# Eight token subtractions moved from GpSimd to VectorE, two issue paces changed, and the last short block's sum taken off the accumulating DMA

## The chip, the cores and the metric

The kernel runs on one core of one Trainium2 chip. The metric is the device time of one execution in microseconds (us), the median of several runs. The engines are called PE (TensorE), DVE (VectorE), ACT (ScalarE), POOL (GpSimd) and SP (SyncE, which issues most DMAs).

## The reference, cut to what matters

Three stages follow each other over 2304 tokens of width 512. A linear attention gives `x`. A gated MLP (GLU) with 1536 hidden features replaces it:

```python
xn = x / rms * rms_g
x = (silu(xn @ w_gate) * (xn @ w_val)) @ w_out
```

A plain MLP with 2048 hidden features ends it. The change lies almost wholly in this last stage:

```python
h = x @ w_in
out = silu(h) @ w_out
```

Everything is float32. The weights come as float64 and are decoded on the chip.

## The kernel before, in words

**Blocks.** The tokens lie in five blocks: 0 to 3 of 512 tokens and a short one, 4, of 256. Every float32 operand of a product is held as a high and a low half (the high half is an ACT copy to the matmul type, the low half a DVE subtraction, lines 198 and 199 for `h`), and a product runs three passes, `PASS`.

**Groups of hidden features.** `stream()` goes through `groups`: nine GLU groups of one feature tile each, then eight MLP groups of a pair of feature tiles. The first two MLP groups (here the first and second pair; `NSTD = 2`) are computed plainly, block by block, with `mlp_block` and `g1_mlp`. From the third pair on, the four long blocks go through `quad`, which forms a pair of blocks and a pair of feature tiles with seven half products instead of eight, in the manner of Strassen. For that, `quad` wants sums and differences of the two blocks of a pair ("token sums") and of the two weight tiles. Behind the two quads of a group come the short block's two products and the output rows of block 3.

**Token sums.** `token_sums(p, ...)` returns a list of small steps for block pair `p`: four additions of 128x1024 elements on DVE (`whole`, line 371), four subtractions on POOL (`less`, line 341), four high halves on ACT (`tok_high`, line 363) and four low halves on DVE (`tok_low`, line 366). It is called once for the GLU and, for the MLP, once for pair 0 in the middle of the first plain group and once for pair 1 in the middle of the second. A step that is not done when `quad` needs its result is issued there (`summed`).

**Weights.** `WeightQueue` holds jobs in a fixed order: load a float64 tile, decode it (five DVE instructions, lines 146 to 157, then two POOL additions, line 160), high half on ACT (line 438), low half on DVE (line 442), weight sums on POOL, and so on. `tick()` issues the next job if a weight slot is free. `quad` calls it at fixed places; elsewhere the loop at the end of the kernel calls it by pace. `need` issues jobs at once if a product wants a weight that is not ready.

**The pacing loop.** The stream yields an estimate of TensorE time before each product and behind each output slice (about 1.3 for a half product or an output slice of 128 tokens, 2.6 for a whole product of a long block). The loop adds it to two counters:

```python
for c in stream():
    due += c
    gone += c
    if sums and gone > wq.rest:
        sums.pop(0)()
        gone = 0.0
    if wq.hold:
        due = min(due, M_PACE)
    elif due > wq.pace and wq.tick():
        due = min(due - wq.pace, wq.pace)
```

`wq.rest` spaces the token sum steps, `wq.pace` the weight jobs. `wq.hold` is on inside a quad. `gone` is reset only where a step is issued, so it goes on growing while the list of sums is empty.

**Outputs.** `g2_mlp` computes output rows for 128 tokens at a time. Even slices leave PSUM by ACT (line 316), odd ones by DVE (line 318), and a pair is added to `out` in HBM by an accumulating DMA that POOL issues (line 323). In the last group, block 2 comes last: its rows so far are loaded from `out` beforehand (line 815), DVE adds the PSUM result to them (line 310), and SP writes them with plain DMAs (line 312); its last slice is cut in two halves. Block 4, just ahead of it, still goes by the accumulating DMA.

Of the kernel before, what the change touches and what calls it, by code (L numbers as in the profile page):

```python
# [8 lines left out]
F32 = mybir.dt.float32  # L9
# [5 lines left out]
ALU = mybir.AluOpType  # L15
# [5 lines left out]
def kernel(  # L21
# [14 lines left out]
    nc = tc.nc  # L36
# [8 lines left out]
    TB = 4  # L45
# [144 lines left out]

    PASS = [(0, 0), (0, 1), (1, 0)]
    HALVES = [slice(0, 64), slice(64, P)]
    M_PACE, A_PACE, S_PACE, R_PACE, T_PACE = 2.0, 1.8, 2.5, 1.5, 1.2
    W_EARLY, GRAIN, GATE = 3, 3, 3

    def split_h(s, j):
# [82 lines left out]
    def out_pair(j, n):  # L279
        i = j * TB + 2 * n  # L280
        kind, b, hf, r = tiles[i]
        if kind == "m":
            r0 = b * S + 256 * hf
            return [(0, P, out[r0:r0 + 256, :].rearrange("(p r) d -> p r d", r=2))]
        rows = out.rearrange("(b s) d -> s b d", s=S)[512:576]
        return [(64 * e, 64 * e + 64, rows[:, e::2, :]) for e in range(2)]

    def g2_mlp(fs, j, hs, first, last, end):
        wq.need(*[(2, "p", f) for f in fs])
        nt = blocks[j] // P  # L290
        nn = 3 * len(fs)
        cuts = [(t, 0, DM) for t in range(nt)]
        if end:
            cuts[-1:] = [(nt - 1, d, d + DM // 2) for d in (0, DM // 2)]
        for t, d0, d1 in cuts:
            ps = ps_tile("ps_y", [P, DM])[:, d0:d1]
            n = 0
            for f in fs:
                for a, c in PASS:
                    nc.tensor.matmul(  # L300
                        out=ps,
                        lhsT=hs[f][:, a, t * P:(t + 1) * P],
                        rhs=wt[2, "p", f][:, c, d0:d1],
                        start=(n == 0),
                        stop=(n == nn - 1),
                    )
                    n += 1
            if end:
                o = end[t // 2][:, t % 2, d0:d1]
                nc.vector.tensor_tensor(out=o, in0=ps, in1=o, op=ALU.add)  # L310
                for p0, p1, rows in out_rows(j * TB + t):
                    nc.sync.dma_start(out=rows[:, d0:d1], in_=o[p0:p1])
            else:
                if t % 2 == 0:
                    o = stage()
                    nc.scalar.activation(out=o[:, 0, :], in_=ps, func=AF.Copy)  # L316
                else:
                    nc.vector.tensor_copy(out=o[:, 1, :], in_=ps)  # L318
                    for p0, p1, rows in out_pair(j, t // 2):
                        if first:  # L320
                            nc.sync.dma_start(out=rows, in_=o[p0:p1])
                        else:
                            nc.gpsimd.dma_start(out=rows, in_=o[p0:p1], accum_op=ALU.add)  # L323
            yield 0.216 * nn

    KH = KC // 2
    tok, sums, ready, wait, stages = {}, [], set(), [], []
# [8 lines left out]
    def w_tile(side, slot, dtype=F32R):  # L336
        pool = pools["w"][2] if side and slot < W_EARLY else pools["w"][side]
        return pool.tile([P, 2 * KC * P], dtype, tag=f"w{side}_{slot}", name=f"w{side}_{slot}")

    def less(out, x, y, op=ALU.subtract):  # L340
        nc.gpsimd.tensor_tensor(out=out, in0=x, in1=y, op=op)
# [3 lines left out]
            sums.pop(0)()  # L345
        return lambda b, c: tok[p, n][b][:, c, :]

    def token_sums(p, temp, end):
        half = lambda j, a, h: xs[2 * p + j][:, a, KH * h:KH * (h + 1), :].bitcast(F32)
        u = {}  # L350

        def tok_high(n, x):
            if n == 1:
                tok[p, n] = [xs[2 * p + 1][:, a, :KH, :] for a in range(2)]
            elif p:
                v = big.tile([P, KC * TB * P], F32R, tag=f"ya{n - 2}", name=f"ya{n - 2}")
                v = v.rearrange("p (a c t) -> p a c t", a=2, c=KH)
                tok[p, n] = [v[:, a] for a in range(2)]
            else:
                tok[p, n] = [  # L360
                    w_tile(1, 3 + 2 * (n - 2) + a).rearrange("p (c t) -> p c t", c=KH) for a in range(2)
                ]
            nc.scalar.activation(out=tok[p, n][0], in_=x, func=AF.Copy)

        def tok_low(n, x):
            nc.vector.tensor_tensor(out=tok[p, n][1], in0=x, in1=tok[p, n][0].bitcast(F32), op=ALU.subtract)
            ready.add((p, n))

        def whole(k, j, h):
            u[k] = u[1] if k == 3 else temp(k).rearrange("p (c t) -> p c t", c=KH)  # L370
            nc.vector.tensor_tensor(out=u[k], in0=half(j, 0, h), in1=half(j, 1, h), op=ALU.add)

        ready.difference_update([(p, n) for n in range(1, 5)])
        return [
            lambda: whole(1, 1, 0),
            lambda: whole(0, 0, 0),
            lambda: less(u[0], u[1], u[0]),
            lambda: whole(2, 1, 1),
            lambda: less(u[1], u[2], u[1]),
            lambda: less(u[2], u[2], u[0]),  # L380
            lambda: tok_high(3, u[1]),
            lambda: (tok_low(3, u[1]), tok_high(2, u[2])),
            lambda: tok_low(2, u[2]),
            lambda: whole(3, 0, 1),
            lambda: less(u[3], u[3], u[2]),
            lambda: None,
            lambda: tok_high(4, u[3]),
            lambda: (tok_low(4, u[3]), end(0)),
        ], [
            lambda: tok_high(1, u[0]),  # L390
            lambda: (tok_low(1, u[0]), end(1)),
        ]
# [173 lines left out]
    wq = WeightQueue()  # L566
# [147 lines left out]
    def chain_of(*its):  # L714
        for it in its:
            yield from it

    def stream():
# [10 lines left out]
            wq.hold = n == 0  # L729
            wq.rest = T_PACE if wq.hold else M_PACE + T_PACE  # L730

        now, later = token_sums(0, temp, end)
        sums.extend(now)
        for n, (j, fs) in enumerate(order):
            hs, mine = {}, n == len(order) - 1
# [6 lines left out]
            out = g2_glu(fs, j, hs, j >= NE and fs is f0, False)  # L742
            pend = chain_of(pend, out) if mine else out
        spent = [(1, k) for k in range(3)]
        for u, (kind, fs) in enumerate(groups):
            first, last = kind == 2 and fs[0] == 0, u == len(groups) - 1
            done = u + 1 == std
            wq.rest = T_PACE + M_PACE / 2
            wq.pace = A_PACE if u < std else S_PACE if u < std + NSTD else R_PACE
            hs = {j: {} for j in range(NB)}  # L750
            if std <= u < std + NSTD:
                out_of = lambda j: g2_mlp(fs, j, hs[j], first, False, False)
# [7 lines left out]
                for n, k in enumerate(each):  # L760
# [11 lines left out]
                    j = n // 2 if first else 1 - n // 2  # L772
                    yield from mlp_block(fs[n % 2], j, hs[j], ys, k if n < 3 else (k[0], 9))
                wq.hold = False
                if first:
                    assert wq.jobs.pop(0)[0] == 1 << 10
                    now, later = token_sums(
                        0, lambda k: w_tile(1, 7, F32) if k == 2 else wq.slot(("t", k), F32), lambda n: None
                    )
# [17 lines left out]
            if kind == 1:  # L797
                f = fs[0]
                out_of = lambda j: g2_glu(fs, j, hs[j], False, done)
                ys = chain_of(out_of(0), out_of(1))  # L800
                yield from glu_block(f, 2, hs[2], ys, {"g": 0, "v": 1})
                yield from glu_block(f, 3, hs[3], ys, {"g": 1, "v": 1})
                yield from glu_block(f, 4, hs[4], ys, {"g": 1, "v": 1})
                yield from ys
                pend = chain_of(out_of(2), out_of(3), out_of(4))
                wq.release(*wq.keys(u)[0])
            else:
                out_of = lambda j, end=None: g2_mlp(fs, j, hs[j], False, last, end)
                yield from quad(u, chain_of(out_of(1), out_of(0)), hs, 1)
                if last:  # L810
                    *stages[:], o0, o1 = [w_tile(1, k, F32) for k in range(3, 9)]
                    ends = [o.rearrange("p (t d) -> p t d", t=2) for o in (o0, o1)]
                    for n, o in enumerate(ends):
                        for p0, p1, rows in out_pair(2, n):
                            nc.sync.dma_start(out=o[p0:p1], in_=rows)
                    yield from g1_mlp(fs[0], 4, hs[4], (), out_of(3))
                    yield from g1_mlp(fs[1], 4, hs[4], (), ())
                    yield from chain_of(out_of(4), out_of(2, ends))
                else:
                    yield from g1_mlp(fs[0], 4, hs[4], (), out_of(3))  # L820
                    yield from g1_mlp(fs[1], 4, hs[4], (), ())
                    wq.release(*wq.keys(u)[0])
                    pend = chain_of(out_of(2), out_of(4))
# [697 lines left out]
    with tc.manual_schedule():  # L1521
# [68 lines left out]
        for c in stream():  # L1590
            due += c
            gone += c
            if sums and gone > wq.rest:
                sums.pop(0)()
                gone = 0.0
            if wq.hold:
                due = min(due, M_PACE)
            elif due > wq.pace and wq.tick():
                due = min(due - wq.pace, wq.pace)
# [30 lines left out]
```

## Time and profile before

| | us |
|---|---|
| median of 3 runs | 970.9 |
| lowest and highest of them | 969.96, 971.26 |
| the profiled execution, its own time | 971.98 |
| its span, first to last instruction | 970.2 |
| PE busy with matmuls | 941.4 (97%) |
| DVE busy | 709.1 (73%) |
| POOL busy | 473.0 (49%) |
| ACT busy | 473.4 (49%) |

The profiled execution's own time is 1.8 us more than its span, and 1.1 us above the median of the runs. The granted TensorE clock has a mean of 0.994 of full speed. The chain of work that ended last lies on PE for 82% of the span and on DVE for 9%. From 236 to 556 us (the GLU groups) PE has no idle time; the MLP's two plain groups lie from about 556 to 664 us, its six quad groups from there to 963 us.

### The profile page before, as it was taken

What the parts mean: (1) busy time and instruction counts of PE and PEld (TensorE: products, weight loads), DVE (VectorE), ACT (ScalarE), POOL (GpSimd) and SP (SyncE); (2) the same over time, 40 slices, a digit from 0 to 9 for tenths busy, and PEclk for the clock granted to TensorE, in tenths of its full rate; (3) what the DMA queues carried; (4) which work ended last, traced back from release to release, by engine and by line L of the source; (5) the groups of instructions that cost most, each with busy time, mean ns of one, the idle gap of its engine ahead of it and who ended that gap; (6) DMA issues with size and microseconds to landing.
All of it is one profiled execution on the core that took longest, in us unless ns stands there. A gap on an engine that the chain in (4) does not pass through costs nothing.

```text
span 970.2 us, 17242 instructions
## 1 busy us (share of the span) xinstructions
PE 941.4 (97%) x6534; PEld 786.3 (81%) x6534; DVE 709.1 (73%) x1336; ACT 473.4 (49%) x1052; POOL 473.0 (49%) x474
## 2 busy tenths in 40 slices
PE   8999999999999999999999999989899999999996
PEld 6888878888888888888888877778688877878785
DVE  5998989658678777878877879778586747474633
ACT  5999876543433343333332453435445454545441
POOL 7888655315436534534534106386364546363411
PEclk9999999999999999999999999999999999999998
DMA  7655543002112112012102004475777877686667
GB/s 176 174 135 144 139 124 100 5 31 80 44 44 66 33 55 66 22 44 66 44 22 87 23 22 129 133 129 105 134 137 147 153 130 170 112 172 112 111 130 149
DMA packets 88962, 94.50 MB, mean 97 GB/s; under 512 B 28336, under 2 KB 74672, under 8 KB 88880
## 3 DMA queue, kind: packets, MB, share of 16 engines
q1 hardware_dynamic: 78816, 61.36, 22.4%
q0 software_dynamic: 9792, 31.99, 20.0%
q8 instruction: 51, 0.84, 0.4%
q14 instruction: 31, 0.25, 0.1%
q10 hardware_dynamic: 272, 0.07, 0.0%
HBM read 50.92 MB, written 37.75 MB: 91 GB/s over the span
## 4 chain that ended last, share of the span: by engine, by line
PE 82%; DVE 9%; DMA 2%; issue 2%; ACT 2%; POOL 2%; SPq 1%; DVEq 0%; POOLq 0%; ACTq 0%
PE g L572 19%; PE g L205 16%; PE y L300 16%; PE y L259 13%; PE y L205 5%; PE b L1098 3%; PE b L205 2%; DVE h L199 2%; PE b L1282 2%; PE kv L1178 2%; PE b L1071 2%; PE b L1498 1%; POOL m L160 1%; DVE w L442 1%; PE b L1258 1%
## 5 line engine op out<-in xcount | busy, mean ns | idle before, releaser
L160 POOL TENSOR_TENSOR m<-m,raw 128x512 int32<-128x512 int32 x136 | 192.4, 1415 | 211.9 <-issue 118.5
L300 PE MATMUL y<-w,h 128*128 128x512 f32 (+1 forms) x870 | 216.6, 393 | 9.6 <-DVE h L199 4.6
L300 PEld LDWEIGHTS y<-w,h 128*128 128x128 f32 x870 | 163.4, 190 | 46.8 <-DVE h L199 6.0
L205 PE MATMUL g<-xs,w 128*128 128x512 f32 x768 | 187.4, 390 | 1.4 <-DVE w L442 1.4
L205 PEld LDWEIGHTS g<-xs,w 128*128 128x128 f32 x768 | 143.3, 188 | 31.1 <-DVE w L442 1.9
L199 DVE TENSOR_TENSOR h<-s,h 128x512 fp32r<-128x512 f32 (+1 forms) x134 | 110.0, 831 | 63.9 <-ACT h L198 62.7
L259 PE MATMUL y<-h,w 128*128 128x512 f32 (+1 forms) x648 | 155.4, 366 | 0.0
L270 DVE TENSOR_TENSOR ya<-y,ya 128x512 f32<-128x512 f32 (+1 forms) x200 | 122.7, 630 | 21.0 <-PE y L259 20.8
L259 PEld LDWEIGHTS y<-h,w 128*128 128x128 f32 x648 | 113.2, 188 | 20.4 <-DVE h L199 0.5
L572 PE MATMUL g<-xs,w 128*128 128x512 f32 x504 | 128.7, 391 | 0.0
L198 ACT ACTIVATE h<-s 128x512 fp32r<-128x512 f32 (+1 forms) x134 | 77.3, 585 | 89.7 <-DVE s L684 49.4
L323 POOL DMA_DIRECT2D out_dram<-ya x64 | 59.3, 989 | 117.9 <-DVE ya L318 55.1
L572 PEld LDWEIGHTS g<-xs,w 128*128 128x128 f32 x504 | 94.3, 188 | 19.5
L318 DVE COPY ya<-y 128x512 f32<-128x512 f32 x67 | 45.9, 686 | 71.1 <-PE y L300 71.1
L1147 ACT ACTIVATE e<-b,nb 128x128 f32<-128x128 f32 x272 | 75.8, 421 | 7.9 <-issue 4.3
L442 DVE TENSOR_TENSOR w<-m,w 128x512 fp32r<-128x512 f32 x65 | 70.7, 1088 | 11.9 <-ACT w L438 10.7
L316 ACT ACTIVATE ya<-y 128x512 f32<-128x512 f32 x67 | 39.8, 593 | 71.4 <-PE y L300 70.3
L572 PE MATMUL g<-w,w 128*128 128x512 f32 x270 | 68.8, 390 | 0.0
L205 PEld LDWEIGHTS y<-xs,w 128*128 128x128 f32 x480 | 61.2, 188 | 8.9 <-ACT ya L316 6.4
L597 ACT ACTIVATE s<-s 128x512 f32<-128x512 f32 x33 | 20.9, 632 | 96.0 <-DVE s L602 96.0
L205 PE MATMUL y<-xs,w 128*128 128x256 f32 x480 | 62.5, 280 | 5.2 <-ACT ya L316 5.2
L572 PEld LDWEIGHTS g<-w,w 128*128 128x128 f32 x270 | 50.1, 188 | 10.0
(135 smaller groups left out, 1352.1 us busy)
## 6 DMA issues: line engine op xcount, KB each, us to landing
out_dram<-ya POOLq DMA_DIRECT2D x52, 512.0 KB, 6.7
raw<-in_moe_w_out_dram SPq DMA_DIRECT2D x28, 512.0 KB, 4.1
raw<-in_moe_w_in_dram SPq DMA_DIRECT2D x16, 512.0 KB, 4.3
raw<-in_moe_w_gate_dram SPq DMA_DIRECT2D x12, 512.0 KB, 3.5
raw<-in_moe_w_val_dram SPq DMA_DIRECT2D x12, 512.0 KB, 3.6
qT<-e SPq DMA_DIRECT2D x72, 64.0 KB, 2.6
x<-in_k_dram SPq DMA_DIRECT2D x16, 256.0 KB, 3.6
x<-in_q_dram SPq DMA_DIRECT2D x16, 256.0 KB, 3.3
```

The costliest lines, as they stand in the source:

```text
L160: tt(out=mi, in0=mi, in1=(low if step == 5 else high).bitcast(I32), op=ALU.add)
L198: nc.scalar.activation(out=ht[:, 0, :], in_=s, func=AF.Copy)
L199: nc.vector.tensor_tensor(out=ht[:, 1, :], in0=s, in1=ht[:, 0, :].bitcast(F32), op=ALU.subtract)
L205: nc.tensor.matmul(out=ps, lhsT=w[:, a, cc * P:(cc + 1) * P], rhs=xs[j][:, c, cc, :], start=(n == 0), stop=(n == 3 * KC - 1),)
L259: nc.tensor.matmul(out=ps, lhsT=wt[1, "o", f][:, a, d * P:(d + 1) * P], rhs=hs[f][:, c, :], start=(n == 0), stop=(n == nn - 1),)
L270: nc.vector.tensor_tensor(out=y[:, d, :], in0=ps, in1=y[:, d, :], op=ALU.add)
L300: nc.tensor.matmul(out=ps, lhsT=hs[f][:, a, t * P:(t + 1) * P], rhs=wt[2, "p", f][:, c, d0:d1], start=(n == 0), stop=(n == nn - 1),)
L318: nc.vector.tensor_copy(out=o[:, 1, :], in_=ps)
L323: nc.gpsimd.dma_start(out=rows, in_=o[p0:p1], accum_op=ALU.add)
L442: eng.tensor_tensor(out=v[:, 1, :], in0=x, in1=v[:, 0, :].bitcast(F32), op=ALU.subtract)
L572: nc.tensor.matmul(out=ps, lhsT=w[:, a, (c0 + c) * P:(c0 + c + 1) * P], rhs=x(b, c), start=(start and n == 0), stop=(n == 3 * KH - 1), ski ...
L1147: nc.scalar.activation(out=st.e[r][:, :, h, :] if blocks4 else st.e[r][:, h, :], in_=src.rearrange("p (a f) -> p a f", a=4) if blocks4 els ...
```

## The change

It moves the four subtractions of each of the MLP's two `token_sums` calls from POOL to DVE (the GLU's stay on POOL). It sets the spacing of the sum steps to 1.9 in place of 2.2 and keeps what is left of `gone` behind a step in place of setting it to zero. It sets the pace of weight jobs in the quad groups to 2.0 in place of 1.5. In the last group the short block's rows are loaded, added on DVE and written by SP as block 2's are.

```diff
-    M_PACE, A_PACE, S_PACE, R_PACE, T_PACE = 2.0, 1.8, 2.5, 1.5, 1.2
+    M_PACE, A_PACE, S_PACE, R_PACE, S_REST, T_PACE = 2.0, 1.8, 2.5, 2.0, 1.9, 1.2
...
-        if end:
+        if end and nt == TB:
             cuts[-1:] = [(nt - 1, d, d + DM // 2) for d in (0, DM // 2)]
...
-    def token_sums(p, temp, end):
+    def token_sums(p, temp, end, eng=nc.vector):
...
+        def minus(out, x, y):
+            eng.tensor_tensor(out=out, in0=x, in1=y, op=ALU.subtract)
+
...
-            lambda: less(u[0], u[1], u[0]),
+            lambda: minus(u[0], u[1], u[0]),
             lambda: whole(2, 1, 1),
-            lambda: less(u[1], u[2], u[1]),
-            lambda: less(u[2], u[2], u[0]),
+            lambda: minus(u[1], u[2], u[1]),
+            lambda: minus(u[2], u[2], u[0]),
...
-            lambda: less(u[3], u[3], u[2]),
+            lambda: minus(u[3], u[3], u[2]),
...
-        now, later = token_sums(0, temp, end)
+        now, later = token_sums(0, temp, end, nc.gpsimd)
...
-            wq.rest = T_PACE + M_PACE / 2
+            wq.rest = S_REST
...
-                    *stages[:], o0, o1 = [w_tile(1, k, F32) for k in range(3, 9)]
-                    ends = [o.rearrange("p (t d) -> p t d", t=2) for o in (o0, o1)]
-                    for n, o in enumerate(ends):
-                        for p0, p1, rows in out_pair(2, n):
+                    *stages[:], o0, o1, o2 = [w_tile(1, k, F32) for k in range(3, 9)]
+                    ends = [o.rearrange("p (t d) -> p t d", t=2) for o in (o0, o1, o2)]
+                    for o, j, n in zip(ends, (4, 2, 2), (0, 0, 1)):
+                        for p0, p1, rows in out_pair(j, n):
                             nc.sync.dma_start(out=o[p0:p1], in_=rows)
...
-                    yield from chain_of(out_of(4), out_of(2, ends))
+                    yield from chain_of(out_of(4, ends[:1]), out_of(2, ends[1:]))
...
-                gone = 0.0
+                gone = gone - wq.rest if wq.rest == S_REST else 0.0
```

## Rows read from the trace of the kernel before

**Rows 1.** Busy time in stretches: start:end, length, busy by engine, PE clock, DMA

```profile
556.00:664.00 108.00, 100.38 (x461) 82.95 (x460) 88.63 (x117) 47.23 (x82) 50.17 (x31) 0.98 0.36 93
664.00:712.00 48.00, 44.95 (x194) 36.34 (x193) 31.21 (x47) 23.16 (x39) 22.34 (x20) 0.96 0.74 137
```

**Rows 2.** What PE waited for, 575 to 963 us: total, times, longest

```profile
PE y L205 <- ACT ya L316: 5.2, 3, 1.7
PE y L300 <- DVE h L199: 4.6, 2, 2.5
PE y L300 <- DVE w L442: 2.9, 2, 2.7
PE y L300 <- DVE ya L270: 1.6, 1, 1.6
PE g L205 <- DVE w L442: 1.4, 1, 1.4
```

**Rows 3.** DVE in order of time, 582 to 603 us: start, us, what, idle before

```profile
582.03 0.68 DVE L199 TENSOR_TENSOR h<-s,h 128x512 fp32r<-128x512 f32 x1
582.63 1.22 DVE L371 TENSOR_TENSOR w<-xs 128x1024 f32<-128x1024 f32 x1
583.76 0.42 DVE L146 TENSOR_SCALAR m<-raw 128x512 uint32<-128x512 uint32 x1
...
585.10 0.42 DVE L157 TENSOR_SCALAR m<-m 128x512 uint32<-128x512 uint32 x1
586.86 0.69 DVE L318 COPY ya<-y 128x512 f32<-128x512 f32 x1 [1.33 <-PE y L300]
587.46 1.97 DVE L371 TENSOR_TENSOR w<-xs 128x1024 f32<-128x1024 f32 x1
...
595.28 5.65 DVE L199 TENSOR_TENSOR h<-s,h 128x512 fp32r<-128x512 f32 x2
```

**Rows 4.** POOL in order of time, 584 to 604 us

```profile
585.65 2.69 POOL L160 TENSOR_TENSOR m<-m,raw 128x512 int32<-128x512 int32 x2 [40.63 <-issue]
...
594.23 8.95 POOL L341 TENSOR_TENSOR w<-w,w 128x1024 f32<-128x1024 f32 x3
```

**Rows 5.** PE in order of time, 594 to 613 us

```profile
598.18 4.64 PE L300 MATMUL y<-w,h 128*128 128x512 f32 x19 [2.07 <-DVE h L199]
...
610.29 1.19 PE L205 MATMUL g<-xs,w 128*128 128x512 f32 x4 [1.45 <-DVE w L442]
```

**Rows 6.** All engines in order of time, 627 to 647 us

```profile
628.39 1.22 DVE L366 TENSOR_TENSOR xs<-w,xs 128x1024 fp32r<-128x1024 f32 x1
...
636.83 3.52 POOL L160 TENSOR_TENSOR m<-m,raw 128x512 int32<-128x512 int32 x2 [0.67 <-DVE m L157]
...
639.14 1.76 DVE L199 TENSOR_TENSOR h<-s,h 128x512 fp32r<-128x512 f32 x1
...
640.96 6.12 PE L300 MATMUL y<-w,h 128*128 128x512 f32 x19 [2.49 <-DVE h L199]
```

**Rows 7.** PE in order of time, 676 to 698 us

```profile
687.09 0.73 PE L300 MATMUL y<-w,h 128*128 128x512 f32 x2 [2.72 <-DVE w L442]
687.66 1.99 PE L572 MATMUL g<-xs,w 128*128 128x512 f32 x6
689.45 2.71 PE L300 MATMUL y<-w,h 128*128 128x512 f32 x6
692.00 1.55 PE L572 MATMUL g<-ya,w 128*128 128x512 f32 x6
```

**Rows 8.** All engines in order of time, 804 to 811 us

```profile
805.11 3.06 POOL L160 TENSOR_TENSOR m<-m,raw 128x512 int32<-128x512 int32 x2 [2.23 <-issue]
...
808.21 0.63 ACT L438 ACTIVATE w<-m 128x512 fp32r<-128x512 f32 x1 [4.00 <-POOL m L160]
...
808.74 0.58 ACT L316 ACTIVATE ya<-y 128x512 f32<-128x512 f32 x1
...
809.38 1.68 PE L205 MATMUL y<-xs,w 128*128 128x256 f32 x12 [1.72 <-ACT ya L316]
```

**Rows 9.** All engines in order of time, 936 us to the end

```profile
958.76 1.99 POOL L323 DMA_DIRECT2D out_dram<-w  x2 [3.82 <-issue]
...
959.60 5.71 SPq L312 DMA_DIRECT2D out_dram<-w  x5
...
963.03 0.42 DVE L310 TENSOR_TENSOR w<-y,w 128x256 f32<-128x256 f32 x1 [0.29 <-PE y L300]
```

**Rows 10.** Line 312's own view: its issues by SP, and their time to landing

```profile
L312 SPq DMA_DIRECT2D out_dram<-w x5: 332/344/1494, 959.6 to 964.4; - x5
...
DMA to landing us min/median/max: 3.6/4.8/5.8
```

## The prediction

> **What bounds the kernel now.** I read the page's busy times first: PE is busy for 941.4 of 970.2 us, so only its idle time and its slow stretches can be won. Next the busy time by stretches. The GLU groups leave PE no idle time. The two plain MLP groups leave 108 - 100.38 = 7.6 us idle, and the third pair's group 48 - 44.95 = 3.1 us, at a mean clock of 0.98 and 0.96 [rows 1]. Then PE's waits, which name the idle time [rows 2]: 4.6 us for low halves of `h` and 1.4 us for a weight's low half in the plain groups, 2.9 us for weights in the third pair's group, 5.2 us in three equal pieces later, for an ACT copy of `y`. The 1.6 us for `ya` are the last GLU group's, which the change doesn't touch.
>
> DVE holds PE up in the plain groups because POOL holds DVE up. A 128x1024 sum on DVE takes 1.22 us alone (1.13 to the next start), and 1.97 us where it meets POOL's pair of additions: it ends 1.1 us after that pair's end at 588.34 [rows 3, 4]. Two low halves, 0.6 us each when free, take 5.65 us beside POOL's three subtractions of 3.0 us each [rows 3, 4]. So a DVE instruction whose inputs lie in SBUF waits out the POOL instruction that is running, and the two engines take turns. The copy from PSUM at 586.86 isn't held by the same POOL pair. The Trainium skill (SBUF — State Buffer, Who interferes with whom) says the same: a VectorE instruction with two SBUF inputs and a GpSimd instruction that reads SBUF exclude each other for a whole instruction; the rows agree.
>
> **The change part by part.**
>
> *How often sums are issued.* By the text, 1.9 in place of 2.2. But `gone` isn't reset while no sums are pending. By the stream's own estimates it has grown by some 345 through the nine GLU groups when the MLP's first sum becomes ready. A step now takes only 1.9 off it and each yield gives back 1.3 or more, so the 32 steps use up at most 32 x 0.6 = 19. The spacing never bites: one step goes out at every yield, so at half products and output slices (1.3) twice as often as before. Counted along the stream, pair 0's steps end before the second plain group (before: inside it), and pair 1's before the third pair's group (before: inside it).
>
> *First plain group, term +0.4.* Between the first sum (582.63) and the low half PE waits for, DVE's queue now holds three subtractions at 1.13 = 3.4 us more, while POOL's first subtraction, about 2.7 to 3.0 us, no longer stands ahead. I walked the queue in turns: sum, decode (five instructions, 583.76 to 585.52, so 1.75), sum, copy 0.6, subtraction, sum, decode, copy, subtraction, low half 0.6, subtraction, low half, with four POOL additions of 1.35 in between. The second low half ends at 599.3; PE now goes on at 598.2 [rows 5]. The 1.2 us are mostly given back at the next stop, the weight's low half: three DVE steps (a token low half, a sum, a subtraction) now stand ahead of it, and two POOL subtractions don't. I get 610.7 against 610.3 [rows 5]. Bounds: -3.4 (both stops, 2.07 + 1.45, go) and +1.7.
>
> *Second plain group, term +3.6.* The stop before 640.96 waits for the low half at 639.14 [rows 6]. Before, DVE needs from the token low half at 628.39 to 640.9 for it: that low half, two decodes, two copies, two sums and the half itself, with four POOL additions in turn. Afterwards the token low half starts about 3.3 us earlier, at 625.1. But a weight's and an `h` low half (1.2) now follow it, and one sum and three subtractions more stand ahead of the half PE wants: 4 x 1.13 = 4.5, and 0.7 of waiting for ACT. 640.9 - 3.3 + 1.2 + 4.5 + 0.7 = 644.0, so 3.1 us later. Behind the stop PE's 19 matmuls took 6.12 us, against 4.64 for 19 after the first stop [rows 5, 6]: the granted clock drops for a while (the two stretches with such stops have means under 1 [rows 1]), which costs some 1.5 to 1.8 us; I add 0.5 for a longer stop. Bounds: -4.2 (the 2.49 us stop and its slow stretch go, if the turns with POOL cost less than walked) and +5.
>
> *Third pair's group, term -4.6.* The two stops (2.9 us) wait for low halves of the output weights [rows 2, 7]. They are late because two weight slots serve as scratch for pair 1's sums until these end: along the stream, the weight jobs find no slot free five times. With the sums done earlier only one attempt fails, and both weights are split before their product. What goes with the stops is the slow stretch behind: the two groups of six after 687.66 take until 692.00 [rows 7], with the two matmuls before them 4.9 us for 14 that take 3.2 at full clock, so 1.7 us. Bounds: 0 and -4.9.
>
> *Pace of weight jobs, term -5.2.* Behind the quads lie six yields of 1.3. With 1.5 four jobs go out in the first four, so a weight's high half reaches ACT while POOL still decodes: ACT waits 4.0 us for POOL, the copy of `y` behind it comes at 808.74, and PE, which wants that PSUM bank, stops for 1.72 us [rows 8]; three groups have this, 5.2 us [rows 2]. With 2.0 the jobs go out at yields 1, 2, 4 and 5, and the high half comes behind the copy that PE wants, one slice later. Each group issues 14 jobs, ten at fixed places in the quads and four here, before as after, so the jobs in the quads move by one place and none is forced. Their cover is the quads' slack: before, PE waits for nothing in them from 712 us on. If a moved decode does strike a low half there, it costs one turn, 1.35 us a group. Bounds: 0 and -5.5.
>
> *The end, term -0.7.* PE's order is the same to its last matmul. Two more DVE adds take the place of an ACT and a DVE copy; two POOL accumulating DMAs (958.76 to 960.75) go, and four SP writes and two loads come [rows 9]. The added writes are issued before 959.6, while SP has nothing to do; at 0.34 each [rows 10] they cost 1.4 us of its queue, hidden there. The loads run 25 us ahead. What ends the span is the last write, issued at 964.4, landing up to 5.8 us later, where the quickest takes 3.6 [rows 10]. Less beside it may win up to 2.2 us; one SP issue took 1.49, and four such would cost 1 us at the end. I take a third of the gain.
>
> Sum: 0.4 + 3.6 - 4.6 - 5.2 - 0.7 = -6.5. The profiled execution's 971.98 becomes 965.5; it stood 1.1 above the median, so the median of 970.9 becomes **964.4**.
>
> **The rivals.**
>
> *DVE is eased more than I walked.* POOL's subtractions blocked DVE by up to 3 us each and DVE's cost 1.13. If the turns with POOL's decodes overlap more with copies than I let them, the stops of the plain groups shrink: without them and the slow stretch, -7.6 in place of +4.0, so 952.8; half of that 958.6. For it: DVE is busy 88.63 of 108 us there, including its waits [rows 1]. Against: the sums now go out in bursts.
>
> *The third group or the boundary stops stay.* They would if another late job took their place: 964.4 + 4.6 = 969.0, or + 5.2 = 969.6. For it: ACT and POOL stay in order. Against: the count of jobs above.
>
> *Moving work between DVE and POOL wins nothing.* Here the plain groups would stay as they are, the sums' order included, and the rest would come: 964.4 - 4.0 = 960.4. The Trainium skill (Perfetto Trace Analysis, Optimizing Scalar/DVE Operations) warns that shifting operations between these two might not help since they share a read port. It lies inside my range.
>
> *Slower: the burst in the second plain group.* All 14 steps of pair 1 go out at 1.3 us of PE time apart, together with two decodes and `h`. If each low half of `h` there, not only the first, comes behind a sum and a POOL turn, three more stops of 2.5 us with a slow stretch of 1.8 each follow: 3 x 4.3 = 12.9, so 977.3. It decides from about 8.4 us of such stops on, two of them. Against: from 644 us on the sums still left are six DVE steps, 7 us, over more than 20 us of PE time.
>
> **How the numbers follow.** My forecast has 0.55, the eased DVE 0.19, the stops that stay 0.13, no gain from moving 0.06, the slower burst 0.07. The forecast's own bounds reach about 961 to 968. The range goes from 957.5, the better half of the eased case, to 970.0 beyond the stops that stay. A measurement of this kernel tells about 0.2%, 1.9 us, from no change, so faster means below 969.0: the forecast, the eased case, the useless move and about a third of the stops that stay, 0.83; within, 0.10; slower, 0.07.
>
> **What would show it.** In the changed profile: no 128x1024 subtraction on POOL after 236 us; sum steps at every yield; PE's stop before 641 us longer, near 5.5 us, and again a slow stretch; no wait for a weight in the third pair's group; none for the ACT copy of `y` at the groups' ends; no accumulating DMA after 955 us. I am wrong if the plain groups get shorter, if the three pieces of 1.7 us stay, or if new waits stand inside the quads.

## The result and the profile after

The changed kernel takes **959.73 us** (median of 4 runs, 959.17 to 960.5), the kernel before, beside it, 971.08 (4 runs, 969.96 to 971.91): a ratio of 0.9884, 95% interval 0.9867 to 0.9902, so 11.3 us less, where 6.5 were forecast. 959.73 lies inside the range. The profiled execution of after took 960.5, with a span of 958.7 against 970.2.

To see where the time went I cut the span at four places of PE's order. The rows of after, PE in order of time:

```profile
575.14 5.69 PE L300 MATMUL y<-w,h 128*128 128x512 f32 x24 [1.63 <-DVE ya L270]
...
664.61 2.99 PE L205 MATMUL y<-xs,w 128*128 128x256 f32 x24
...
712.84 1.58 PE L205 MATMUL y<-xs,w 128*128 128x256 f32 x12
...
944.97 1.58 PE L205 MATMUL y<-xs,w 128*128 128x256 f32 x12
```

They are the MLP's first output products, the short block's products that end the second plain group, and the short block's second product behind the third and behind the last quads. In the kernel before they start at 575.65, 660.51, 713.90 and 952.66. So the lengths in the profiled executions are, in us:

| stretch | before | after | change | forecast |
|---|---|---|---|---|
| two plain groups | 84.86 | 89.47 | +4.61 | +4.0 |
| third pair's group | 53.39 | 48.23 | -5.16 | -4.6 |
| the five groups after it | 238.76 | 232.13 | -6.63 | -5.2 |
| from there to the end | 17.54 | 13.73 | -3.81 | -0.7 |

The rest of the 11.5 us between the spans, 0.5, lies before these products. Three terms came within 1.5 us; the end won five times its forecast. The busy times by stretch, in the columns of [rows 1], show the same trade:

```profile
556.00:664.00 108.00, 98.90 (x429) 80.65 (x428) 88.94 (x126) 46.47 (x78) 32.73 (x22) 0.95 0.35 93
664.00:712.00 48.00, 47.92 (x229) 40.02 (x228) 32.08 (x51) 24.65 (x44) 24.38 (x23) 1.00 0.73 142
```

The plain groups lost 1.5 us of PE's busy time and 0.03 of clock; the third pair's group has no idle time left and full clock. PE's waits, 575 to 963 us, as in [rows 2]:

```profile
PE y L300 <- DVE h L199: 6.6, 3, 4.2
PE y L300 <- DVE ya L270: 1.6, 1, 1.6
PE y L300 <- ACT h L198: 1.1, 2, 0.8
```

All weight waits (2.9 and 1.4 us) and the three for the copy of `y` (5.2 us) are gone; the wait for `h`'s low halves grew from 4.6 to 6.6. Where it stands, PE in order of time:

```profile
596.59 0.96 PE L300 MATMUL y<-w,h 128*128 128x512 f32 x3 [1.70 <-DVE h L199]
598.32 6.20 PE L300 MATMUL y<-w,h 128*128 128x512 f32 x19 [0.78 <-DVE h L199]
...
609.91 1.55 PE L205 MATMUL g<-xs,w 128*128 128x512 f32 x6
...
638.82 0.73 PE L300 MATMUL y<-w,h 128*128 128x512 f32 x2 [0.84 <-ACT h L198]
643.72 7.43 PE L300 MATMUL y<-w,h 128*128 128x512 f32 x19 [4.16 <-DVE h L199]
```

The stop before 643.72 is the one before 640.96 [rows 6], now 4.16 us. What DVE does before it, in order of time:

```profile
624.95 1.22 DVE L366 TENSOR_TENSOR xs<-w,xs 128x1024 fp32r<-128x1024 f32 x1
...
628.37 2.35 DVE L371 TENSOR_TENSOR w<-xs 128x1024 f32<-128x1024 f32 x2
...
632.32 1.22 DVE L374 TENSOR_TENSOR w<-w,w 128x1024 f32<-128x1024 f32 x1
...
634.05 1.74 DVE L371 TENSOR_TENSOR ya<-xs 128x1024 f32<-128x1024 f32 x1
...
638.53 1.21 DVE L374 TENSOR_TENSOR w<-ya,w 128x1024 f32<-128x1024 f32 x1
...
640.27 1.71 DVE L374 TENSOR_TENSOR ya<-ya,w 128x1024 f32<-128x1024 f32 x1
641.90 1.76 DVE L199 TENSOR_TENSOR h<-s,h 128x512 fp32r<-128x512 f32 x1
```

Six 128x1024 sums and subtractions (line 374 holds the latter) stand between the token low half and the low half that PE wants: the burst. Between the corresponding rows of before [rows 6], DVE has two sums:

```profile
632.54 1.37 DVE L371 TENSOR_TENSOR w<-xs 128x1024 f32<-128x1024 f32 x1
...
637.26 1.95 DVE L371 TENSOR_TENSOR w<-xs 128x1024 f32<-128x1024 f32 x1
```

POOL's decode pair beside those of after:

```profile
638.70 4.41 POOL L160 TENSOR_TENSOR m<-m,raw 128x512 int32<-128x512 int32 x2 [0.67 <-DVE m L157]
```

It takes 4.41 us, against 2.69 when DVE lets it run [rows 4]: taking turns costs POOL as well. Behind the short block's first product of a quad group, all engines in order of time (the place of [rows 8]):

```profile
801.81 0.60 ACT L316 ACTIVATE ya<-y 128x512 f32<-128x512 f32 x1 [1.18 <-PE y L300]
...
802.30 0.62 ACT L441 ACTIVATE w<-m 128x512 fp32r<-128x512 f32 x1
...
803.32 3.02 POOL L160 TENSOR_TENSOR m<-m,raw 128x512 int32<-128x512 int32 x2 [2.23 <-issue]
...
804.53 0.60 ACT L316 ACTIVATE ya<-y 128x512 f32<-128x512 f32 x1 [1.60 <-PE y L300]
```

The weight's high half (line 441) now stands behind a copy of `y`, and the next copy waits for PE alone, not for POOL. The end, DVE's last row and line 312's own view:

```profile
955.36 0.42 DVE L310 TENSOR_TENSOR w<-y,w 128x256 f32<-128x256 f32 x1 [0.29 <-PE y L300]
```

```profile
L312 SPq DMA_DIRECT2D out_dram<-w x9: 332/372/588, 949.2 to 955.8; - x9
...
DMA to landing us min/median/max: 1.8/2.7/3.3
```

The last write is issued 0.4 us after the start of the last add (before: 1.3), and lands after 1.8 us (before: 3.6; the least in each view [rows 10]); the median landing is 2.7 us against 4.8. The rest lies behind the last landing: from it to the end of the span pass 1.1 us, before 2.3. There each engine closes the program with a `DRAIN`, and POOL's is the long one. First before, then after (of three, the shortest, middle and longest in ns, then the first and last start in us; the longest is the first):

```profile
L1625 POOLq DRAIN  x3: 40/102/10253, 959.2 to 969.9; - x3
...
L1628 POOLq DRAIN  x3: 40/93/8527, 946.4 to 958.4; - x3
```

In before it runs from 959.2 for 10.25 us, to 969.4: 2.8 us behind the landing of the last accumulating DMA (issued at 959.4, landed 7.2 us later), and 1.5 behind that of the last plain write, at 967.9. So there the span waited for POOL, not for the last write. In after POOL's `DRAIN` ends at 954.9, ahead of the last write's landing at 957.6. The pieces are 0.9, 1.8 and 1.2 us, together the 3.8 but for rounding.

### The profile page after: what moved, and what is told of

It is laid out like the page before. It is cut to its first block, busy times and chain, and to the rows that moved or that the text cites. A ratio compares the mean times of both kernels' runs of the same rounds, so it can differ in the third digit from the quotient of the medians.

```text
span 958.7 us, 17244 instructions
## 1 busy us (share of the span) xinstructions
PE 940.8 (98%) x6534; PEld 787.4 (82%) x6534; DVE 718.9 (75%) x1345; ACT 474.3 (49%) x1051; POOL 454.9 (47%) x464
## 4 chain that ended last, share of the span: by engine, by line
PE 80%; DVE 4%; ACT 1%; issue 0%; ACTq 0%
PE g L575 21%; PE y L300 20%; PE g L205 16%; PE y L259 13%; PE y L205 6%; PE b L1501 2%; PE b L205 1%; DVE h L199 1%; DVE w L374 1%; PE b L1285 1%; DVE w L371 0%; ACT h L198 0%; PE b L1381 0%; DVE ya L270 0%; ACT xs L272 0%
## 5 line engine op out<-in xcount | busy, mean ns | idle before, releaser
L160 POOL TENSOR_TENSOR m<-m,raw 128x512 int32<-128x512 int32 x136 | 196.4, 1444 | 242.7 <-issue 113.6
L199 DVE TENSOR_TENSOR h<-s,h 128x512 fp32r<-128x512 f32 (+1 forms) x134 | 117.8, 890 | 61.6 <-ACT h L198 60.5
L445 DVE TENSOR_TENSOR w<-m,w 128x512 fp32r<-128x512 f32 x65 | 67.1, 1034 | 17.9 <-ACT w L441 16.2
```

The lines of the kernel that those rows point to most:

```text
L160: tt(out=mi, in0=mi, in1=(low if step == 5 else high).bitcast(I32), op=ALU.add)
L199: nc.vector.tensor_tensor(out=ht[:, 1, :], in0=s, in1=ht[:, 0, :].bitcast(F32), op=ALU.subtract)
L445: eng.tensor_tensor(out=v[:, 1, :], in0=x, in1=v[:, 0, :].bitcast(F32), op=ALU.subtract)
```

## The experiments

Ratios are to the kernel before on the same chip, whose medians there are 969.55 to 971.06. The edits are to the kernel after unless said otherwise. The stretches of the table above, for all of them, are those of one profiled execution each; the medians are of four runs, in x1_pool and x2_pace of seven:

| kernel | plain | third | five groups | end | median, us | ratio (95%) |
|---|---|---|---|---|---|---|
| x1_pool | 93.00 | 52.94 | 232.13 | 13.68 | 967.51 | 0.9964 (0.9948 to 0.9980) |
| x2_pace | 87.95 | 47.95 | 240.98 | 13.70 | 967.81 | 0.9967 (0.9954 to 0.9981) |
| x3_tail | 89.03 | 47.84 | 232.13 | 17.61 | 962.91 | 0.9920 (0.9905 to 0.9935) |
| x4_reset | 80.78 | 53.34 | 256.44 | 13.70 | 981.76 | 1.0115 (1.0098 to 1.0132) |
| x5_early | 90.05 | 47.84 | 232.13 | 13.75 | 958.90 | 0.9874 (0.9857 to 0.9890) |
| x6_acclate | 89.32 | 48.24 | 232.14 | 17.65 | 963.34 | 0.9924 (0.9907 to 0.9940) |
| x7_nodebt | 84.03 | 47.84 | 232.13 | 13.70 | 953.93 | 0.9833 (0.9814 to 0.9852) |
| x8_comb | 86.77 | 47.85 | 232.13 | 13.69 | 955.66 | 0.9849 (0.9830 to 0.9868) |
| x9_paceonly | 84.12 | 53.80 | 256.13 | 17.35 | 988.28 | 1.0186 (1.0167 to 1.0204) |
| x10_split | 83.13 | 47.84 | 232.14 | 13.78 | 951.92 | 0.9804 (0.9787 to 0.9820) |
| x11_split2 | 82.62 | 48.10 | 232.13 | 13.75 | 953.57 | 0.9822 (0.9805 to 0.9839) |

**x1_pool: the subtractions back on POOL.**

```diff
-    def token_sums(p, temp, end, eng=nc.vector):
+    def token_sums(p, temp, end, eng=nc.gpsimd):
```

> The changed kernel with the MLP's eight subtractions back on POOL, all else as changed. Theory (DVE and POOL take turns, a POOL subtraction holds DVE 2.7 us where DVE's own takes 1.13): the plain groups get longer by 1 to 5 us, so 961 to 965 us against 959.7, likeliest 962. Rival (moving work between the two wins nothing): within 1 us of 959.7. Rival (the burst on DVE is what lengthens the plain groups): 956 to 958.

Measured: 967.51, beyond the range; the move to DVE is worth 7.8 us under the burst; of the profiled executions' difference 3.5 lie in the plain groups and 4.7 in the third pair's group, which I had not foreseen. Its waits:

```profile
PE y L300 <- DVE h L199: 8.4, 5, 3.3
PE g L205 <- DVE w L445: 3.1, 1, 3.1
PE g L575 <- ACT g L587: 2.4, 1, 2.4
```

POOL's subtractions take 2.6 to 2.8 us each here, so the sums end inside the third group: the last token low half runs on DVE at 674.33 to 676.66, a weight's high half on ACT waits for it, and the ACT copy that PE wants (line 587) comes behind. "Moving work between DVE and POOL wins nothing" falls.

**x2_pace: the pace of weight jobs back to 1.5** (`R_PACE`).

> The changed kernel with the pace of weight jobs in the quad groups back at 1.5. Theory (at 1.5 a weight's high half stands ahead of the copy that PE wants): the 1.7 us stops for ACT come back. Counted along the stream, the jobs now stand so that four groups have the bad order, not three, at 1.9 to 2.2 us each: 967.3 to 968.5 us. Rival (the stops went because the third pair's jobs are early, not by the pace): 959.7 to 961.5 us, no such stop.

Measured: 967.81, 8.1 us more than after, with four stops of the kind of [rows 8], 6.9 us in all, at 761.66, 810.06, 858.47 and 906.88. One of them:

```profile
810.06 1.68 PE L205 MATMUL y<-xs,w 128*128 128x256 f32 x12 [1.72 <-ACT ya L316]
```

The pace removes them; what it is worth here is 8.85 us of the five groups.

**x3_tail: block 4 of the last group back on the accumulating DMA** (the two hunks of `g2_mlp` and of the last group's loads undone).

> The changed kernel with block 4 of the last group back on the accumulating DMA. Theory (the accumulating DMA beside the last writes delays them): the time from PE's last matmul to the end goes back from 3.4 to about 7 us, 963 to 964 us. Rival (the end got shorter for another reason, for example SP's queue or an earlier end): 959.5 to 960.7 us.

Measured: 962.91, with an end of 17.61, before's 17.54 again: the whole term of the end belongs to this edit. Line 312's writes land in 3.8 to 5.9 us, one write's issue takes 1.302, and POOL's `DRAIN` ends at 960.3, 1.5 us behind the last write's landing.

**x6_acclate: what about the accumulating DMA costs.** Block 2's first pair of slices goes by it, block 4 stays on plain writes.

```diff
-            if end:
-                o = end[t // 2][:, t % 2, d0:d1]
+            if end and end[t // 2]:
+                o = end[t // 2][0][:, t % 2, d0:d1]
...
-                    ends = [o.rearrange("p (t d) -> p t d", t=2) for o in (o0, o1, o2)]
-                    for o, j, n in zip(ends, (4, 2, 2), (0, 0, 1)):
+                    ends = [[o.rearrange("p (t d) -> p t d", t=2)] for o in (o0, o1, o2)]
+                    for (o,), j, n in zip(ends[::2], (4, 2), (0, 1)):
...
+                    ends[1] = None
```

> The changed kernel with the first half of block 2's last rows (tokens 0 to 255 of it) on the accumulating DMA again, block 4 on plain writes, so one accumulating DMA of 512 KB is issued about 2.5 us before PE's last matmul. Theory (an accumulating DMA under way makes the last plain writes land later): median landing of the plain writes over 3.5 us, against 2.7, and the end 1 to 4 us later: 960.7 to 963.7 us. Rival (the number of writes or SP's queue sets the landing): landing at most 2.7 us, end no later than the accumulating DMA's own landing.

Measured: 963.34, as x3_tail, end 17.65; the four runs fall in two pairs, near 961.9 and 964.8, and the profiled one is of the upper pair. POOL issues that DMA at 954.15, and only the writes behind it are late, so the median over all seven stays at 2.9. Line 312 from 953.5 us on, x6_acclate:

```profile
L312 SPq DMA_DIRECT2D out_dram<-w x3: 350/405/683, 955.0 to 956.2; - x3
...
DMA to landing us min/median/max: 4.5/4.8/4.9
```

and in after, from 953 us on:

```profile
L312 SPq DMA_DIRECT2D out_dram<-w x4: 332/341/361, 953.3 to 955.8; - x4
...
DMA to landing us min/median/max: 1.8/2.1/2.3
```

An accumulating DMA issued in the last microseconds makes the last plain writes land 2.7 us later, whichever block it carries. But the span waits for that DMA itself, longer than for the writes. It lands at 959.4, the last plain write at 960.6, and POOL's `DRAIN` ends at 962.2, 0.8 us before the span:

```profile
L1629 POOLq DRAIN  x1: 8097/8097/8097, 954.1 to 954.1; - x1
```

**x4_reset: the old spacing of the sums** (2.2, counter set to zero), with all else of the change.

```diff
-    M_PACE, A_PACE, S_PACE, R_PACE, S_REST, T_PACE = 2.0, 1.8, 2.5, 2.0, 1.9, 1.2
+    M_PACE, A_PACE, S_PACE, R_PACE, S_REST, T_PACE = 2.0, 1.8, 2.5, 2.0, 2.2, 1.2
...
-                gone = gone - wq.rest if wq.rest == S_REST else 0.0
+                gone = 0.0
```

> The changed kernel with the sum steps spaced as before (2.2, counter set to zero behind a step); subtractions on DVE, pace 2.0 and the new end stay. Theory: the burst alone made the plain groups longer, and the early end of the sums alone took the third group's stops away. So the plain groups get shorter than before the change (stops of about 1 and 2.5 us, some 7 us less than as changed) and the third group's stops of about 5 us with their slow stretch come back: 956 to 960 us, likeliest 957.9. Rival (the third group's stops went because the subtractions left POOL): no such stop, 952 to 954 us.

Measured: 981.76, slower than before. The plain groups did as expected (80.78, 4.1 below before's), but the late weights of the third group come back in every group (in the last only 0.64 us). PE in order of time:

```profile
681.71 0.73 PE L300 MATMUL y<-w,h 128*128 128x512 f32 x2 [2.72 <-DVE w L445]
...
733.76 0.95 PE L300 MATMUL y<-w,h 128*128 128x512 f32 x2 [3.74 <-DVE w L445]
...
785.85 1.22 PE L300 MATMUL y<-w,h 128*128 128x512 f32 x2 [3.73 <-DVE w L445]
```

The stop at 681.71 is the one of [rows 7]. In the kernel before it doesn't recur, at pace 1.5. A group needs 14 jobs. The quads have ten fixed places. Behind them `due` starts from 2.0, where `wq.hold` clamps it, and six yields of 1.3 follow: by the loop that makes four places at pace 2.0 and six at 1.5. So 1.5 has two spare places with which jobs that failed for want of a slot catch up, and 2.0 has none.

**x9_paceonly: the kernel before with the pace alone at 2.0.**

> The kernel before with the pace of weight jobs in the quad groups at 2.0 and nothing else. Theory (at 2.0 a group has as many chances as jobs, 14, so jobs that lost five chances to the late sums are late in every group from the third pair on): the three stops for ACT go, but PE waits 3 to 4 us for a weight's low half with a slow stretch in each of four or five groups: 983 to 989 us, slower than before. Rival (the jobs catch up within the third pair's group): 964 to 966 us.

Measured: 988.28, as expected: 18.7 us slower than before (969.55 beside it). Its waits for weights are those of x4_reset to the digit:

```profile
PE y L300 <- DVE w L442: 18.5, 7, 3.7
```

So the pace is worth -8.1 us with the sums done early (x2_pace) and +18.7 without. Nor is it enough that the third group is late: in x1_pool it takes 52.94 us, but steps and jobs are *issued* in after's order, no job is missing, and the five groups take 232.13.

**x5_early: the fourth block of the second plain group split ahead of its output slices**, to bring the low half forward that PE stops for.

```diff
-            yield from take(ys, n[k])
+            if k == 0 or not early:
+                yield from take(ys, n[k])
...
         hs[f] = split_h(s, j)
+        if early:
+            yield from take(ys, n[1])
```

> The changed kernel, but in the second plain group the fourth block's activation and split are issued ahead of the four output slices instead of behind them, so that the low half PE stops for stands ahead of the sums in DVE's queue. Theory (PE's stop before 644 us is this low half waiting behind a decode, a sum and two subtractions): both pieces of the stop (0.8 and 4.2 us) and the slow stretch behind it (about 3 us) go: 950.5 to 953.5 us. Rival (DVE has too much to do there in any order): the stop moves to the next low half or to a copy, 955.5 to 959.7 us.

Measured: 958.9, not told apart from after. The stop moves on to the next low half and grows:

```profile
654.80 6.82 PE L300 MATMUL y<-w,h 128*128 128x512 f32 x22 [5.87 <-DVE h L199]
```

DVE is busy without a gap from 628 to 654 us there: with the burst in its queue, the order of one half changes nothing.

**x7_nodebt: the spacing as its text says**, 1.9, with the counter held at zero while no sum is pending.

```diff
-            gone += c
+            gone = gone + c if sums else 0.0
```

> The changed kernel with the counter for the sum steps kept at zero while no sums are pending, so that they really go out 1.9 apart and not at every yield. Theory (the credit saved up during the GLU groups makes the burst, and the burst makes PE's stops in the plain groups long): the stop before 644 us falls from 5.0 to about 3.5 us with a shorter slow stretch, and so does the one before 598; pair 1's sums still end soon enough that at most three weight jobs find no slot: 954 to 958 us. Rival (every later weight job is lost for good, as with the spacing of before): late weights in the third pair's group and all after it, 970 us or more.

Measured: **953.93**, 5.8 us below after, or 5.0 by the ratios, since the kernel before takes 969.55 beside it. DVE before the stop of the second plain group, and then PE behind it:

```profile
624.32 1.22 DVE L366 TENSOR_TENSOR xs<-w,xs 128x1024 fp32r<-128x1024 f32 x1
...
627.14 1.22 DVE L371 TENSOR_TENSOR w<-xs 128x1024 f32<-128x1024 f32 x1
...
628.87 1.73 DVE L371 TENSOR_TENSOR w<-xs 128x1024 f32<-128x1024 f32 x1
...
633.95 1.94 DVE L374 TENSOR_TENSOR w<-w,w 128x1024 f32<-128x1024 f32 x1
635.80 1.76 DVE L199 TENSOR_TENSOR h<-s,h 128x512 fp32r<-128x512 f32 x1
...
637.62 5.97 PE L300 MATMUL y<-w,h 128*128 128x512 f32 x19 [3.21 <-DVE h L199]
```

Three sums and subtractions where after has six, and a stop of 3.21 us for 4.16: the counter's growth through the GLU groups is real. The plain groups are 5.4 us shorter in the profiled execution, which is the fastest of the four. The sums still end before the third pair's group (47.84).

**x8_comb: x7_nodebt with splits ahead of the output slices in both plain groups, and their odd copies on ACT.**

> As the run with the counter kept at zero, and in the plain groups the fourth block's and block 2's first split ahead of the output slices beside them, and all copies of output slices of the first two pairs on ACT, which is half idle there. Theory (DVE's load in the two plain groups is the bound, some 26 us of work for 23 us of PE time before PE wants the low half of block 2's second feature tile): 0.6 us for each copy taken off DVE and the earlier low halves leave stops of at most 3 us in all: 949 to 954 us. Rival (ACT becomes the bound: its copies wait for POOL and for sums in order): new waits for ACT, 956 us or more.

Measured: 955.66, no gain over x7_nodebt. ACT now has the queue that is late: its row for a weight's high half waits 5.82 us for POOL, with `h` and the copies behind, and PE stops 3.3 us for ACT's `h`:

```profile
640.00 0.63 ACT L447 ACTIVATE w<-m 128x512 fp32r<-128x512 f32 x1 [5.82 <-POOL m L160]
```

```profile
630.73 9.23 POOL L160 TENSOR_TENSOR m<-m,raw 128x512 int32<-128x512 int32 x2 [16.47 <-DVE m L157]
```

POOL's pair took 9.23 us, 3.4 times the 2.69 of [rows 4]. From 630.51 to 637.42 DVE runs ten instructions (a low half, four sums and subtractions, a decode) without a gap, each at its free duration, and, its copies being on ACT, without a copy from PSUM. The first of POOL's two additions, 1.3 us when free, ends only at 638.59.

**x10_split and x11_split2: the splits alone.** x10_split is x7_nodebt with x5_early's edit; x11_split2 adds the same to block 2 in both plain groups (`g1_mlp`).

```diff
-                    yield from mlp_block(fs[n % 2], j, hs[j], ys, k if n < 3 else (k[0], 9))
+                    yield from mlp_block(fs[n % 2], j, hs[j], ys, k if n < 3 else (k[0], 9), n == 3 and not first)
...
-            gone += c
+            gone = gone + c if sums else 0.0
```

> Base: the kernel after with the counter of the sum spacing held at zero while no sum is pending (x7_nodebt), plus the fourth block of the second plain group split ahead of its output slices (as in x5_early). Theory: with the sums really 1.9 apart DVE has gaps in the second plain group, so an earlier split is an earlier low half, and x7's stop of 3.21 us and its slow stretch (5.97 in place of 4.61 us for 19 matmuls) go: 953.9 - 4.6 = 949.3, so 949 to 951.5. Rival: as in x5_early the wait moves on to the next low half of h; then the time is x7's or above it, 953 to 957, with a stop of 3 us or more before another product's output slices.

> x10_split plus the same early split of block 2 in the plain groups (x8_comb without its ACT copies). Theory: the low halves of block 2 come ahead of the copies of the late output slices, and what is left of the small stops of the first plain group (0.56, 0.77 and 0.49 us in x7) shrinks: x10's time less 0 to 1.5 us. Rival: x8_comb lost by its earlier splits, not by its copies on ACT: then ACT's or DVE's h is waited for behind block 2 for 3 us or more, as there (3.5 and 3.0 us), and the time is 954 to 957.

Measured: **951.92** and 953.57. The first lies between the theory's range and the rival's; the second, not below the first, is nearer its rival's. Both beat the kernel before and after clearly; their intervals overlap each other's and x7_nodebt's, so a gain of the splits isn't shown. In x10_split's profiled execution, the slowest of its four, the stop shrinks to 1.31 us, but moves on as the rival has it, and the clock falls behind it; in x11_split2's, the fastest of its four, a longer stop has no such cost. PE in order of time, x10_split and then x11_split2:

```profile
648.87 6.22 PE L300 MATMUL y<-w,h 128*128 128x512 f32 x19 [1.31 <-DVE h L199]
```

```profile
648.97 4.60 PE L303 MATMUL y<-w,h 128*128 128x512 f32 x19 [2.64 <-DVE h L199]
```

## Why the prediction was right, and where it wasn't

**The range: in part luck.** 959.73 lies below the 961 that the forecast's own terms reach. It is in the range because that went down to 957.5 for an eased DVE, which didn't come; what did come is a larger gain at the end.

**The burst: right.** Steps at every yield, a longer stop before 641 us and a slow stretch behind it were foretold, and x7_nodebt shows that the uncleared counter is the cause. The stop's size was 4.16 in place of some 5.5, with another of 0.84 ahead of it for ACT's `h`.

**First plain group, +0.4: the sum right, two of its pieces not.** Up to the short block's products it is 2.2 us longer (31.94 against 29.73), and the weight's stop of 1.45 behind them is gone, so +0.8. I had the stop for `h` longer by 1.2 at first: it is 1.70 + 0.78 in place of 2.07, so +0.4. I had not foreseen that 19 matmuls take 6.20 us behind it, against 4.64, nor that the weight's low half comes in time.

**Second plain group, +3.6: right.** 2.40 us longer from short block to short block, and 1.45 of that stretch was the weight's stop before, so +3.85.

**Third pair's group, -4.6: right** (-5.16), for the reason given: no weight wait is left, and the clock is 1.00.

**The pace, -5.2: right in size, its cover named wrongly.** The three stops went, 1.89 us each from the short block's spacing (8.78 before, 6.89 after), so 5.7 of the 6.63. Another 0.75 lies in one group's quads, where before had a stop of 0.17 us for ACT's `h` at 781.15, with slower matmuls behind it; that PE waits for nothing there from 712 us on was not quite so. But the step "their cover: quads' slack; none is forced" left out that the 14 places have no spare. The cover is the third pair's group: with a job behind at its end, the same edit costs 18.7 us (x9_paceonly). I added this term to that of the third group as if the two were independent, and priced the rival in which the third group's stops stay at +4.6; x4_reset, which keeps them by issuing the sums late, stands 22 us above after. That was the real slower case, and the one I named instead, three more stops of a burst, didn't come.

**The end, -0.7: the mis-sized term**, measured -3.81, outside my bound of -2.2. The step that failed is "what ends the span is the last write", with the quickest landing, 3.6, as a floor. That 3.6 is the last write's own, at 967.9; the 5.8 is another's. The span waited for POOL's `DRAIN`, until 969.4, and all five landings lay behind or beside accumulating DMAs. Without these in the last microseconds the wait for POOL goes (1.2), the last write lands in 1.8 (so another 1.8), and it is issued 0.9 sooner; x3_tail and x6_acclate bring the long end back with the DMA. This makes 3.1 of the 4.8 us by which the change did better than forecast.

**The rivals of the useless move and of the eased DVE.** The warning of the Trainium skill (Perfetto Trace Analysis, Optimizing Scalar/DVE Operations) that moving operations between VectorE and GpSimd might not help isn't borne out here: a 128x1024 subtraction is 1.2 to 2.0 us on DVE (after) and 2.6 to 2.8 on POOL (x1_pool), and the move wins 3.3 us in the plain groups at the old spacing (84.12 in x9_paceonly, 80.78 in x4_reset) and 7.8 in all under the burst. The "eased" rival's half step, 958.6, lies nearest to the result, but its reason is wrong: the plain groups got longer.

**What stays open.** What decides whether the clock drops behind a stop, and when POOL gets its turn beside DVE (both below); and what the best order of `h` in the plain groups is.

## What to carry to other kernels

A counter that paces work must be stopped while there is nothing to pace, or the first steps come out in one burst; one line won some 5 us here. A pace with no spare place works only as long as nothing upstream is late, so cost such edits together with what keeps them fed, not as a sum of parts. Take the floor of a latency from a row in which the suspected load is absent; if there is none, the gain may exceed every bound read from the loaded rows. And look for what ends the span: here it was not the last write but the closing of the engine that had issued the slower DMA.

## What the runs showed of the hardware that was not expected

**Plain writes behind an accumulating DMA.** They land in 4.5 to 4.9 us against 1.8 to 2.3 for the last writes without one (x6_acclate, after). A plain write issued while such a DMA is under way lands 0.2 to 0.4 us behind it, and the next ones 0.3 to 0.5 apart: in before the DMA at 966.60 and the writes at 966.81, 967.26, 967.60 and 967.93, in x6_acclate the DMA at 959.44 and the writes at 959.88, 960.29 and 960.65. One SP issue beside them took 1.3 us in x3_tail and 1.5 in before, against at most 0.6 in after.

**POOL's closing `DRAIN`.** In all thirteen traces it ends 2.7 to 2.8 us behind the landing of the last accumulating DMA. Where that DMA is issued among the last writes (before, x3_tail, x6_acclate, x9_paceonly) it outlasts SP's last `DRAIN` by 1.1 to 1.3 us, and the span ends 0.8 us behind it; in the nine others SP's ends last.

**The clock behind a stop.** For the same 19 matmuls behind a stop for `h`, 4.60 us at a granted clock of 1.00 (2.4 GHz) follow a stop of 2.64 (x11_split2), and 6.22 at a mean of 0.73, so partly at 1.2 GHz, follow one of 1.31 (x10_split); x1_pool has 4.60 behind 3.23, x7_nodebt 5.97 behind 3.21. The granted clock is the column behind the five engines' busy times; first x10_split, then x11_split2:

```profile
648.87:655.10 6.23, 6.23 (x20) 4.99 (x21) 6.23 (x11) 1.20 (x2) 1.00 (x2) 0.73 0.43 78
```

```profile
648.97:653.60 4.63, 4.63 (x20) 3.86 (x21) 4.63 (x8) 1.20 (x2) 0.00 (x0) 1.00 0.53 95
```

A stop's length alone doesn't tell whether the 1.3 to 2.8 us come on top. Nor does the kernel: the mean clock of x10_split's four executions is 0.998 (953.16 us, the one above), 1.0, 1.0 and 1.0 (951.28 to 952.47), that of x11_split2's 1.0 (951.88, the one above), 0.998, 0.996 (954.39 and 954.86) and 1.0 (952.76).

**POOL in turns with DVE.** The decode pair takes 2.69 us when DVE lets it run, 4.41 beside two subtractions on DVE, and 9.23 beside seven microseconds of DVE work without a copy from PSUM (x8_comb). So the turns aren't always one instruction each, as I walked them: there POOL's first addition waited out all ten of DVE's. That only a copy from PSUM on DVE, or a gap, lets POOL in isn't the rule: in after POOL's addition from 634.78 to 636.95 waits for the sum that DVE is running (634.05 to 635.79) and then goes ahead of a decode instruction, which takes 1.52 us for 0.42, with no copy between. What decides is open.
